# Backward attention loop: the dQ products of two neighbouring query chunks accumulate in one PSUM bank through zero-padded keys

## The chip, the cores and the metric

The kernel runs on one core of one Trainium2 chip. A core has TensorE (PE, with its weight loads listed apart as PEld), VectorE (DVE), ScalarE (ACT), GpSimd (POOL) and SyncE (SP), which run side by side and wait for each other through semaphores; DMA queues are fed from SP, ACT and POOL. The metric is device time in microseconds. The kernel before took 2488.68 us (median of three runs, 2481.41 to 2490.61).

## The reference, cut to what matters

The reference computes one transformer block with adaptive layer norm and all its gradients by `jax.vjp`. The sequence has 2048 tokens, the width is 512, and attention has 32 heads of 16 numbers each. The part that the change touches is the gradient through

```
scores = jnp.einsum('bhqd,bhkd->bhqk', q, k) * Dh ** (-0.5)
p = _softmax(scores, axis=-1)
o = jnp.einsum('bhqk,bhkd->bhqd', p, v)
```

With dS the gradient of the scores, this needs dQ = scale * dS K, dK = scale * dS^T Q and dV = P^T dO for each head, where P and dS are matrices of 2048 x 2048 that are never stored whole.

## The kernel before, in words

A forward part computes the output and the gradients of the dense layers. Then one backward loop goes over the attention matrices. Heads are taken in 8 groups of four (`hg`). For each group the loop goes over 4 chunks of 512 keys (`kc`), inside these over 4 chunks of 512 queries (`qc`), and inside these over 4 tiles of 128 queries (`qi`). One (hg, kc, qc) is called a block here: 128 blocks `b`, of four units each.

A block contains this work:

- `score` (L1594): 16 matmuls, one for each tile of queries and each head. Four heads lie in four groups of 32 rows. Each writes 128 x 512 scores to one PSUM bank: `psS_A`, `psS_B` or `psS_C`, on the tags `ps0`, `ps1` and `px`, one bank each.
- `expo` (L1600): 16 exponentials on ACT, each reading one such bank.
- `dp_pair` (L1614, L1616): 8 pairs of matmuls of dO with V into two banks (two such pairs of banks take turns), and on DVE one product of 128 x 1024 with the exponentials, which gives dS. The pair takes two of the four row groups: the even pairs of heads 0 and 1, the odd ones of heads 2 and 3.
- `k_quad` (L1654) and `v_quad` (L1663): four matmuls each, one for a head, in four groups of 32 columns, summing dK and dV of a key chunk in one bank, `accVK`. ACT copies it out once every four blocks (L1666).
- The transposes of dS: in even blocks DMA transposes, issued by SP (L1629, L1631), in odd blocks the last unit on PE (`pe_turn`, L1644, into bank C, copied out by ACT at L1760 in the block behind). A block's transposed dS is a tile `dsT`, of which there are three.
- `dq_quad` (L1681): four times four matmuls of a slice of K (32 columns, of which 16 are the head's own) with transposed dS, into one bank `dqacc` on the tag `px`, the same bank as `psS_C` and `ptT`.
- `dq_out` (L1691, L1694, L1699): ACT copies `dqacc` out once a block, to `dQacc` for the first key chunk and otherwise to `dqtmp`, which POOL adds to `dQacc`. `dQacc` has a column for each of the 2048 queries.

The engines' order is written out by hand. Two strings give it: `order_t` for even blocks b (whose predecessor used PE for its last transposes) and `order_n` for odd ones. Every engine takes its own instructions out of the string in that order, and waits in it. `s5` is the score 5 of the block, `e5` its exponential, `D` the next pair of dP matmuls with its DVE product (and with the DMA transposes that it makes possible), `q` the next K or V quad in turn, `t1` and `T1` the PE transposes and their copy, `f` a matmul that only keeps the array busy, `d1` and `d2` two dQ quads each, for the block two before, and `Q` its copy. The string of letters behind the order says which bank each score uses. Loads for the next head group are issued on ACT's queue at fixed counts of `D` (`at`, `plan_head`).

All of K lies in one tile `KS_tok` (16 tiles of 128 keys, 512 columns and 16 columns of zeros), loaded once before the loop from `k_st`.

Of the kernel before, what the change touches and what calls it, by code (L numbers as in the profile page):

```python
# [17 lines left out]
BF = dt.bfloat16  # L18
F32 = dt.float32

P = 128
# [9 lines left out]
QPAD = 528  # L31
# [3 lines left out]
def kernel(  # L35
# [54 lines left out]
    k_st = dram.tile([P, TT, D], BF, name="k_st")  # L90
# [56 lines left out]
    with ExitStack() as ph:  # L147
# [836 lines left out]
        def plan_tasks():  # L984
# [72 lines left out]
            def token_tile(which, g, ti):  # L1057
                key = (which, g)
                if ti == 0:
                    T[key] = cb.tile([P, 4, D], BF, name="tokP", tag=htags[(g if which == 0 else g + 1) % 3])  # L1060
                t = 4 * g + ti
                pt = pools["mm"].tile([P, 4, P], BF, name="ptk", tag="pm")
                for b in range(4):
                    src = sP[:, 4 + 4 * (g % 2) + b, ti * P:(ti + 1) * P] if which == 0 else KTs[b][:, t * P:(t + 1) * P]
                    PE.transpose(pt[:, b, :], src, identb[:])
                gs = slice(4 * g, 4 * g + 4)
                if which == 1:
                    DVE.tensor_copy(T[key][:, ti, :], pt.rearrange("p b q -> p (b q)"))
                    if ti == 3:
                        later(1, sp, k_st[:, gs, :], T[key][:])  # L1070
                else:
                    tok = T[key].rearrange("p t d -> p (t d)").rearrange("p (g t e) -> p g t e", g=HG, t=4)
                    DVE.tensor_copy(tok[:, :, ti, :], pt.rearrange("p b q -> p (b q)").rearrange("p (g e) -> p g e", g=HG))
                    if ti == 3:
                        later(1, sp, q_st.rearrange("g p t e -> p g t e")[:, :, gs, :], tok)
# [142 lines left out]

        def tick():
            unit[0] += 1  # L1220
            run_due()
            flush_sums()
            if dwq and unit[0] >= dwq[0][0]:
                next_chain()
# [8 lines left out]
        def last_chunk(O_c, L, w1T, w2T):  # L1233
# [127 lines left out]
            keep["KS"] = kpool.tile([P, TT, QPAD], BF, name="KS_tok", tag="ks")  # L1361
            POOL.memset(keep["KS"][:, :, D:QPAD], 0.0)
            for i in range(4):
                later(4 + 3 * i, sp, keep["KS"][:, 4 * i:4 * i + 4, 0:D], k_st[:, 4 * i:4 * i + 4, :])
# [171 lines left out]
    KS_tok, dOs_tok = keep["KS"], keep["dOs"]  # L1536
# [11 lines left out]
    with ExitStack() as ph:  # L1548
# [9 lines left out]
        def load_head(hg):  # L1558
            st = dict(hsets[hg % 2])
            st["qz"] = qz[hg % 2]  # L1560
            st["acc"] = stg.tile([P, n], F32, name="dQacc", tag="dQacc", bufs=1)
            st["dq"] = stg.tile([P, n], BF, name="dQst", tag="dQst", bufs=1)
            st["vk"] = stg.tile([P, n], BF, name="vkb", tag="vkb")
            hst[hg] = st
# [13 lines left out]
        def plan_head(hg):  # L1578
            j0 = (hg - 1) * 128 + 14
            loads = list(kvq_loads(hg)) + list(row_loads(hsets[hg % 2]["do"], dOT_st, hg, slice(0, n), d_st))  # L1580
            for i, (to, fro) in enumerate(loads):
                at(j0 + 4 * i, load, to, fro)
            at(j0 + 40, spread_qz, hg)

# [51 lines left out]
        def keep_warm():  # L1636
            PE.matmul(cur["vk"][0:DH, :], KS_tok[:, 0, D:QPAD], dOs_tok[:, 0, :], start=False, stop=False,
                      tile_position=(0, 0), skip_group_check=True)
# [34 lines left out]
        def dq_quad(b, kt):  # L1673
            hg, kc, qc, _ = units[4 * b]
            if kt == 0:
# [3 lines left out]
            for hq in range(4):  # L1679
                h = hg * 4 + hq  # L1680
                PE.matmul(acc[32 * hq:32 * hq + 32, :], KS_tok[:, kc * 4 + kt, h * DH:h * DH + 32], tT[:, :, hq * 4 + kt, :],  # L1681
                          start=(kt == 0), stop=(kt == 3), tile_position=(0, 32 * hq), skip_group_check=True)

        def dq_out(b):
            hg, kc, qc, _ = units[4 * b]
            acc = cur["dq"]
            del dqt[b]
            st = hst[hg]
            dst = st["acc"][:, qc * 512:(qc + 1) * 512]
            if kc == 0:  # L1690
                ACT.activation(dst, acc[:], AF.Identity, scale=SCALE)  # L1691
            else:
                tmp = wk.tile([P, 512], F32, name="dqtmp", tag="dqtmp")
                ACT.activation(tmp[:], acc[:], AF.Identity, scale=SCALE)  # L1694
                if kc == QC - 1:
                    dst2 = st["dq"][:, qc * 512:(qc + 1) * 512]
                else:
                    dst2 = dst
                POOL.tensor_tensor(dst2, dst, tmp[:], ALU.add)  # L1699
            if kc == QC - 1 and qc == QC - 1 and hg < HG - 1:  # L1700
                for hq in range(4):
                    r = hg % 2 * 64 + hq * DH
                    at(cur["j"] + 6 + hq, load, dQc[hg // 2, r:r + DH, :], st["dq"][32 * hq:32 * hq + DH, :])
# [4 lines left out]
            "s11 e10 D d1 d2 e11 Q q s12 D e12 s13 e13 q s14 D e14 "  # L1708
            "s15 q q e15 ").split(), "ABCABBABACABABCA"
        order_n = (  # L1710
            "s0 D s1 q e0 q s2 e1 e2 D s3 s4 q s5 e3 D e4 "
            "e5 s6 q s7 D s8 e6 e7 d1 e8 s9 D d2 e9 q Q s10 "
            "s11 e10 D q s12 e11 e12 s13 e13 D q s14 s15 e14 e15 D q ").split(), "CBACBACBABABCABC"
# [6 lines left out]
        with tc.manual_schedule(engines={PE.engine, ACT.engine, DVE.engine, SP.engine, POOL.engine}):  # L1720
# [4 lines left out]
            for b in range(NU // 4 + 3):  # L1725
                toks, bank = order_t if on_pe(b - 1) else order_n
                for tok in toks:
# [33 lines left out]
                    elif c == "d" and 0 <= b - 2 < NU // 4:  # L1761
                        for kt in (2 * i - 2, 2 * i - 1):
                            dq_quad(b - 2, kt)
                    elif c == "Q" and 0 <= b - 2 < NU // 4:
# [4 lines left out]
    with ExitStack() as ph:  # L1769
# [12 lines left out]
        for h in range(4):  # L1782
            SP.dma_start(out=xs["dq", 3][64 + DH * h:64 + DH * h + DH, :], in_=dq_last[32 * h:32 * h + DH, :])
# [238 lines left out]
```

## Time and profile before

| | |
|---|---|
| times of three runs | 2481.41, 2490.61, 2488.68 us; median 2488.68 |
| profiled execution, first to last instruction | 2501.3 us |
| mean granted TensorE clock | 0.980 of full speed |
| first and last exponential of the backward loop start at | 1115.7 and 2375.6 us |
| exponentials in the loop | 2048, medians 632 to 646 ns by bank |
| copies of `dqacc` | 128 (32 into `dQacc`, 96 into `dqtmp`), medians 597 ns |
| sums of dQ on POOL | 64 and 32, means 1268 and 1270 ns |

The profiled execution was 12.6 us longer than the median of the runs. Durations on ACT overlap: the next activation starts before the last one's recorded end, so the distance of two starts says what one costs, and the durations do not. The same holds for matmuls on PE.

### The profile page before, as it was taken

The page shows a single profiled execution, that of the slowest core. Times are in us where ns is not written, and L with a number is a line of the kernel's source. Part 1 is how long each engine was busy: PE and PEld are TensorE (multiplying, and loading weights), DVE is VectorE, ACT ScalarE, POOL GpSimd, SP SyncE. Part 2 cuts the span into 40 slices and gives each one's busy share as a digit, 9 for nine tenths or more (in the row PEclk, how much of TensorE's full clock was granted, in tenths as well). Part 3 has the DMA queues.
Part 4 walks back from the last instruction along what each step waited for, and adds up shares of the span by engine and source line. Part 5 has one row for each costly group of instructions (what it writes and reads, how often), then busy time and mean ns, then how long its engine had stood idle before and what let it go on. Part 6 is the DMA issues. An engine that isn't in the chain of part 4 may idle for free.

```text
span 2501.3 us, 49888 instructions
## 1 busy us (share of the span) xinstructions
PE 2324.0 (93%) x18948; PEld 783.4 (31%) x19036; DVE 1837.7 (73%) x2377; ACT 2303.7 (92%) x3560; POOL 488.0 (20%) x661
## 2 busy tenths in 40 slices
PE   8899899989998998999999999999999999999989
PEld 3232233223332333443223323233232323332344
DVE  6555354455435444579989999999999999999965
ACT  7999999999998999539999999999999999999944
POOL 2111223323533453110111101111011110110100
PEclk9999999999998999999999999999999999999999
DMA  4468463258546865979999999999999999999984
GB/s 146 130 167 176 144 150 97 88 166 142 98 95 142 151 131 110 256 200 196 201 192 206 199 198 202 196 204 203 205 205 198 205 202 199 200 198 214 201 253 133
DMA packets 1189503, 437.70 MB, mean 175 GB/s; under 512 B 1065867, under 2 KB 1160521, under 8 KB 1188878
## 3 DMA queue, kind: packets, MB, share of 16 engines
q1 hardware_dynamic: 1152414, 389.35, 79.0%
q0 software_dynamic: 19872, 27.09, 6.5%
q10 hardware_dynamic: 16976, 18.07, 2.9%
q8 instruction: 149, 2.44, 0.4%
q14 instruction: 92, 0.75, 0.1%
HBM read 98.30 MB, written 70.80 MB: 68 GB/s over the span
## 4 chain that ended last, share of the span: by engine, by line
ACT 40%; PE 38%; issue 8%; DVE 7%; DMA 3%; SPq 1%; ACTq 1%; POOL 0%; DVEq 0%; another core or an unknown queue 0%; POOLq 0%
ACT E_u L1600 24%; ACT ET L578 12%; PE dqacc L1681 4%; PE psST L576 3%; PE psS_A L1594 3%; PE accVK L1654 2%; PE pm L233 2%; ACT dsT L1760 2%; PE psS_B L1594 2%; PE pdh L1858 2%; PE oacc L592 2%; PE psS_C L1594 2%; PE pwq L1892 2%; PE pm L500 2%; PE pm L410 2%
## 5 line engine op out<-in xcount | busy, mean ns | idle before, releaser
L1616 DVE TENSOR_TENSOR dS_u<-psD_u,E_u 128x1024 bf16<-128x1024 f32 x1024 | 1185.9, 1218 | 77.1 <-PE psD_u L1614 30.2
L578 ACT ACTIVATE ET<-psST 128x1024 bf16<-128x1024 f32 x1024 | 941.9, 1242 | 16.6 <-PE psST L576 16.3
L1600 ACT ACTIVATE E_u<-psS_A 128x512 bf16<-128x512 f32 x768 | 509.9, 664 | 10.8 <-PE psS_C L1594 8.5
L1600 ACT ACTIVATE E_u<-psS_B 128x512 bf16<-128x512 f32 x768 | 503.2, 655 | 10.8 <-DMA dsT<-dS_u 2.7
L1614 PE MATMUL psD_u<-iv,ido 32*128 32x512 bf16 x2048 | 409.1, 388 | 1.5 <-DVE dS_u L1616 1.3
L576 PE MATMUL psST<-qt_sb,kt_sb 32*128 32x512 bf16 x2048 | 313.8, 386 | 48.0 <-ACT ET L578 41.0
L1600 ACT ACTIVATE E_u<-psS_C 128x512 bf16<-128x512 f32 x512 | 334.3, 653 | 3.1 <-PE psS_B L1594 1.1
L1594 PE MATMUL psS_B<-ik,iq 32*128 32x512 bf16 x768 | 296.1, 386 | 11.7 <-ACT E_u L1600 4.4
L1594 PE MATMUL psS_A<-ik,iq 32*128 32x512 bf16 x768 | 294.5, 383 | 11.0 <-DVE dwlast L237 1.0
L1699 POOL TENSOR_TENSOR dQacc<-dQacc,dqtmp 128x512 f32<-128x512 f32 x64 | 81.2, 1268 | 858.8 <-ACT dqtmp L1694 797.4
L1594 PEld LDWEIGHTS <-iq 32*128 32x128 bf16 x2048 | 129.7, 91 | 313.9 <-issue 296.9
L1654 PE MATMUL accVK<-dS_u,qz 128*32 128x512 bf16 x2048 | 213.5, 388 | 0.5 <-PE psD_u L1614 0.2
L592 PE MATMUL oacc<-ET,vaug 128*32 128x512 bf16 x2048 | 207.0, 394 | 3.9 <-DVE ostage L596 3.9
L1663 PE MATMUL accVK<-E_u,dOs_tok 128*16 128x512 bf16 x2048 | 204.5, 388 | 0.0
L1594 PE MATMUL psS_C<-ik,iq 32*128 32x512 bf16 x512 | 194.2, 379 | 4.5
L576 PEld LDWEIGHTS <-kt_sb 32*128 32x128 bf16 x2048 | 84.3, 91 | 328.2 <-issue 306.5
L1681 PE MATMUL dqacc<-dsT,KS_tok 128*32 128x512 bf16 x2048 | 145.7, 382 | 18.8 <-DMA dsT<-dS_u 5.0
L1760 ACT ACTIVATE dsT<-ptT 128x1024 bf16<-128x1024 bf16 x128 | 144.1, 1126 | 13.1 <-PE ptT L1644 12.2
L251 DVE COPY part<-pm 128x512 f32<-128x512 f32 (+2 forms) x106 | 65.2, 615 | 121.9 <-PE pm L233 111.8
L1614 PEld LDWEIGHTS <-ido 32*128 32x128 bf16 x2048 | 105.2, 91 | 101.3 <-issue 94.9
L1654 PEld LDWEIGHTS <-qz 128*32 128x32 bf16 x2048 | 58.5, 94 | 178.0 <-issue 162.9
L1699 POOL TENSOR_TENSOR dQst<-dQacc,dqtmp 128x512 bf16<-128x512 f32 x32 | 40.6, 1270 | 266.1 <-ACT dqtmp L1694 266.1
(415 smaller groups left out, 2688.7 us busy)
## 6 DMA issues: line engine op xcount, KB each, us to landing
p_st<-part POOLq DMA_DIRECT2D x36, 256.0 KB, 4.6
kt_sb<-qkT_st POOLq DMA_DIRECT2D x124, 64.0 KB, 3.0
wA<-in_B_w_dram SPq DMA_DIRECT2D x28, 256.0 KB
wB<-w1T_st SPq DMA_DIRECT2D x21, 256.0 KB
wA<-w2T_st SPq DMA_DIRECT2D x21, 256.0 KB
wB<-in_B_w_dram SPq DMA_DIRECT2D x21, 256.0 KB
p_st<-part POOLq DMA_DIRECT2D x28, 192.0 KB, 4.6
p_st<-part SPq DMA_DIRECT2D x18, 256.0 KB
```

Source lines behind the costliest of these rows:

```text
L576: PE.matmul(ps[:, hi, :], kt_sb[r:r + 32, kt * P:(kt + 1) * P], qt_sb[r:r + 32, :], start=True, stop=True, tile_position=(r, 0))
L578: ACT.activation(ET[:, 2 * pair:2 * pair + 2, :], ps[:], AF.Exp, scale=SCALE)
L592: PE.matmul(oacc[32 * hq:32 * hq + 32, :], lhsT, ET[:, hq, :], start=(kt == 0), stop=(kt == TT - 1), tile_position=(0, 32 * hq), skip_grou ...
L1594: PE.matmul(psS[:], st["q"][r:r + 32, qt * P:(qt + 1) * P], st["k"][r:r + 32, kc * 512:kc * 512 + 512], start=True, stop=True, tile_positi ...
L1600: ACT.activation(bst[u][0][:, hq, :], sst.pop((u, hq))[:], AF.Exp, scale=SCALE)
L1614: PE.matmul(psD[:, hi, :], st["do"][r:r + 32, qt * P:(qt + 1) * P], st["v"][r:r + 32, kc * 512:kc * 512 + 512], start=True, stop=True, til ...
L1616: DVE.tensor_tensor(dS_u[:, 2 * pair:2 * pair + 2, :], psD[:], E_u[:, 2 * pair:2 * pair + 2, :], ALU.mult)
L1654: PE.matmul(cur["vk"][32 * hq:32 * hq + 32, :], hst[hg]["qz"][:, qt, hq, :], bst[u][1][:, hq, :], start=(qt == 0), stop=False, tile_positi ...
L1663: PE.matmul(acc[32 * hq:32 * hq + DH, :], dOs_tok[:, qt, (hg * 4 + hq) * DH:(hg * 4 + hq + 1) * DH], E_u[:, hq, :], start=False, stop=(qt ...
L1681: PE.matmul(acc[32 * hq:32 * hq + 32, :], KS_tok[:, kc * 4 + kt, h * DH:h * DH + 32], tT[:, :, hq * 4 + kt, :], start=(kt == 0), stop=(kt ...
L1699: POOL.tensor_tensor(dst2, dst, tmp[:], ALU.add)
L1760: ACT.activation(dst, pt[:], AF.Identity)
```

## The change

One `dQacc` column now holds two queries. The 32 rows that a head has in `dqacc` are split: 16 rows for the even query chunk, 16 for the odd one. To this end each head's keys are laid out as 16 columns of zeros, 16 columns of keys, 16 of zeros (`KPAD` = 144 for four heads, `kpads`). A dQ quad of an even chunk takes 32 columns that begin with the keys, one of an odd chunk 32 columns that end with them. So the 8 quads of two neighbouring blocks sum into one bank, each adding zeros to the other's rows. One copy on ACT and, where there was one, one sum on POOL follow for both blocks.

- `dq_quad` is called once for each of `d1` to `d8`. All eight stand in `order_n`, that is in odd blocks: `d1` to `d4` for the block three before, `d5` to `d8` for the one two before. `Q` stands once, in `order_n` too. `order_t` has no `d` and no `Q` any more.
- The bank letters change: 4 instead of 3 scores of an even block, and 2 instead of 5 scores of an odd one use bank C.
- `dQacc` and `dQst` are half as wide. A head group's stores of dQ are 8 instead of 4 (`dq_stores`).
- K is stored by head group, and loaded for one group at a time (`ktok`), for the next one while one is worked on. POOL spreads it into the padded layout once for each group (`spread_keys`), into one of two buffers.

The number of matmuls does not change.

```diff
-                if which == 1:
-                    DVE.tensor_copy(T[key][:, ti, :], pt.rearrange("p b q -> p (b q)"))
-                    if ti == 3:
-                        later(1, sp, k_st[:, gs, :], T[key][:])
...
+                tok = T[key].rearrange("p t d -> p (t d)").rearrange("p (g t e) -> p g t e", g=HG, t=4)
+                DVE.tensor_copy(tok[:, :, ti, :], pt.rearrange("p b q -> p (b q)").rearrange("p (g e) -> p g e", g=HG))
+                if ti == 3:
+                    later(1, sp, (k_st if which else q_st).rearrange("g p t e -> p g t e")[:, :, gs, :], tok)
...
+        def split_keys():
+            flat_k = keep["KS"]
+            for i in range(2):
+                ktok.append(flat_k[:, i * TT * 64:(i + 1) * TT * 64].rearrange("p (t e) -> p t e", t=TT))
+                lo = 2 * TT * 64 + i * TT * KPAD
+                kpads.append(flat_k[:, lo:lo + TT * KPAD].rearrange("p (t c) -> p t c", t=TT))
+
+        def spread_keys(hg):
+            to = kpads[hg % 2][:, :, DH:].rearrange("p t (h c) -> p t h c", h=4)[:, :, :, 0:DH]
+            POOL.tensor_copy(to, ktok[hg % 2].rearrange("p t (h d) -> p t h d", h=4))
...
-            keep["KS"] = kpool.tile([P, TT, QPAD], BF, name="KS_tok", tag="ks")
-            POOL.memset(keep["KS"][:, :, D:QPAD], 0.0)
-            for i in range(4):
-                later(4 + 3 * i, sp, keep["KS"][:, 4 * i:4 * i + 4, 0:D], k_st[:, 4 * i:4 * i + 4, :])
+            keep["KS"] = kpool.tile([P, 2 * TT * (64 + KPAD)], BF, name="K_tok", tag="ks")
+            split_keys()
+            POOL.memset(keep["KS"][:, 2 * TT * 64:], 0.0)
+            later(4, sp, ktok[0], k_st[0])
+            later(9, spread_keys, 0)
...
+            at(j0 + 22, load, ktok[hg % 2], k_st[hg])
+            at(j0 + 50, spread_keys, hg)
...
-            if kt == 0:
+            odd = qc % 2
+            if kt == 0 and not odd:
                 cur["dq"] = psx.tile([P, 512], F32, name="dqacc", tag="px")
...
-                h = hg * 4 + hq
-                PE.matmul(acc[32 * hq:32 * hq + 32, :], KS_tok[:, kc * 4 + kt, h * DH:h * DH + 32], tT[:, :, hq * 4 + kt, :],
-                          start=(kt == 0), stop=(kt == 3), tile_position=(0, 32 * hq), skip_group_check=True)
+                lo = 32 * hq + (0 if odd else DH)
+                PE.matmul(acc[32 * hq:32 * hq + 32, :], hst[hg]["kpad"][:, kc * 4 + kt, lo:lo + 32], tT[:, :, hq * 4 + kt, :],
+                          start=(kt == 0 and not odd), stop=(kt == 3 and odd == 1), tile_position=(0, 32 * hq), skip_group_check=True)
...
-            dst = st["acc"][:, qc * 512:(qc + 1) * 512]
+            cols = slice(qc // 2 * 512, qc // 2 * 512 + 512)
+            dst = st["acc"][:, cols]
...
+        def dq_stores(to, fro):
+            for hq in range(4):
+                for half in range(2):
+                    yield (to[hq * DH:hq * DH + DH, :].rearrange("c (a e q) -> c a e q", e=2, q=512)[:, :, half, :],
+                           fro[32 * hq + DH * half:32 * hq + DH * half + DH, :].rearrange("c (a q) -> c a q", q=512))
...
             "s5 s6 e5 f f t2 e6 s7 T2 e7 D s8 e8 D f f s9 e9 q q s10 "
-            "s11 e10 D d1 d2 e11 Q q s12 D e12 s13 e13 q s14 D e14 "
-            "s15 q q e15 ").split(), "ABCABBABACABABCA"
+            "s11 e10 D e11 q s12 D e12 s13 e13 q s14 D e14 "
+            "s15 q q e15 ").split(), "ACBABBABACABCABC"
         order_n = (
             "s0 D s1 q e0 q s2 e1 e2 D s3 s4 q s5 e3 D e4 "
-            "e5 s6 q s7 D s8 e6 e7 d1 e8 s9 D d2 e9 q Q s10 "
-            "s11 e10 D q s12 e11 e12 s13 e13 D q s14 s15 e14 e15 D q ").split(), "CBACBACBABABCABC"
+            "e5 s6 q s7 D e6 s8 d1 e7 s9 d2 e8 s10 D d3 e9 s11 d4 q e10 "
+            "D s12 d5 e11 s13 d6 e12 s14 D d7 q e13 s15 d8 e14 Q e15 D q q ").split(), "ABCABCABABABABAB"
...
-                    elif c == "d" and 0 <= b - 2 < NU // 4:
-                        for kt in (2 * i - 2, 2 * i - 1):
-                            dq_quad(b - 2, kt)
-                    elif c == "Q" and 0 <= b - 2 < NU // 4:
+                    elif c == "d" and 0 <= b - 3 < NU // 4:
+                        dq_quad(b - 3 + (i > 4), (i - 1) % 4)
+                    elif c == "Q" and 0 <= b - 3 < NU // 4:
                         dq_out(b - 2)
```

## The prediction

> **What bounds the kernel now.** I read the engine table of the page first, then busy time by stage over the backward loop, then the timeline of 22 us in the middle of that loop. The first exponential of the loop starts at 1115.7 us and the last at 2375.6 us (the answer on the tile `E_u`): 1260 us for 128 blocks, 19.7 us for a pair. The change touches little outside this stretch.
>
> The page, and one stage of the loop (columns: window, length, then busy us of PE, weight loads, DVE, ACT, POOL, the granted clock, the DMA share, GB/s):
>
> ```profile
> span 2501.3 us, 49888 instructions
> ...
> PE 2324.0 (93%) x18948; PEld 783.4 (31%) x19036; DVE 1837.7 (73%) x2377; ACT 2303.7 (92%) x3560; POOL 488.0 (20%) x661
> ```
>
> ```profile
> 1600.00:1700.00 100.00, 96.04 (x938) 30.03 (x929) 95.35 (x83) 98.67 (x190) 11.62 (x8) 1.00 1.21 201
> ```
>
> Three engines look full here, so busy shares don't say which sets the pace. The timeline does (columns: start, duration, engine, line, operation):
>
> ```profile
> 1700.50 0.60 ACT L1600 ACTIVATE E_u<-psS_C 128x512 bf16<-128x512 f32 x1
> ...
> 1703.60 0.37 PE L1594 MATMUL psS_A<-ik,iq 32*128 32x512 bf16 x1
> ...
> 1704.09 0.61 PE L1681 MATMUL dqacc<-dsT,KS_tok 128*32 128x512 bf16 x8
> 1704.33 0.69 ACT L1600 ACTIVATE E_u<-psS_A 128x512 bf16<-128x512 f32 x1
> ...
> 1704.64 0.38 PE L1594 MATMUL psS_B<-ik,iq 32*128 32x512 bf16 x1
> 1704.64 0.39 PE L1614 MATMUL psD_u<-iv,ido 32*128 32x512 bf16 x2
> ...
> 1704.96 0.61 PE L1681 MATMUL dqacc<-dsT,KS_tok 128*32 128x512 bf16 x8
> 1705.06 0.60 ACT L1600 ACTIVATE E_u<-psS_B 128x512 bf16<-128x512 f32 x1
> ...
> 1705.40 0.39 PE L1654 MATMUL accVK<-dS_u,qz 128*32 128x512 bf16 x4
> 1705.68 0.60 ACT L1694 ACTIVATE dqtmp<-dqacc 128x512 f32<-128x512 f32 x1
> ...
> 1705.72 0.39 PE L1594 MATMUL psS_A<-ik,iq 32*128 32x512 bf16 x1
> ...
> 1706.18 0.59 ACT L1600 ACTIVATE E_u<-psS_A 128x512 bf16<-128x512 f32 x1
> ...
> 1706.65 0.61 ACT L1600 ACTIVATE E_u<-psS_B 128x512 bf16<-128x512 f32 x1
> ...
> 1709.04 0.67 ACT L1600 ACTIVATE E_u<-psS_A 128x512 bf16<-128x512 f32 x1
> ...
> 1709.42 0.59 PE L1614 MATMUL psD_u<-iv,ido 32*128 32x512 bf16 x2
> ...
> 1711.42 1.17 ACT L1760 ACTIVATE dsT<-ptT 128x1024 bf16<-128x1024 bf16 x1
> ...
> 1712.33 0.75 ACT L1600 ACTIVATE E_u<-psS_B 128x512 bf16<-128x512 f32 x1
> ...
> 1716.01 1.05 PE L1681 MATMUL dqacc<-dsT,KS_tok 128*32 128x512 bf16 x16
> ...
> 1716.62 0.80 ACT L1600 ACTIVATE E_u<-psS_B 128x512 bf16<-128x512 f32 x1
> ...
> 1717.16 0.76 ACT L1694 ACTIVATE dqtmp<-dqacc 128x512 f32<-128x512 f32 x1
> ...
> 1717.65 0.75 ACT L1600 ACTIVATE E_u<-psS_A 128x512 bf16<-128x512 f32 x1
> ...
> 1719.84 0.60 ACT L1600 ACTIVATE E_u<-psS_C 128x512 bf16<-128x512 f32 x1
> ```
>
> Read starts against starts. Number the exponentials of a block e0 to e15 and their scores s0 to s15. An odd block (written by `order_n`) runs from 1700.50 to 1709.04, 8.54 us; the even block behind it (`order_t`) to 1719.84, 10.80 us: 19.34 us a pair. From the lines come these prices:
>
> - ACT starts an undisturbed exponential every 0.48 us (1706.18, 1706.65). The copy of `dqacc` holds it 0.50 us (1705.68 to 1706.18), a copy of `ptT` 0.91 us (1711.42 to 1712.33).
> - PE starts a further quad of the same kind 0.22 us after the one before: four quads take 1.05 us, of which the last is a matmul's 0.39, and (1.05 - 0.39)/3 = 0.22. From a score to a quad it takes 0.32 us (1704.64 to 1704.96), from a quad to a score 0.32 us too (1705.40 to 1705.72). Elsewhere in the same timeline both are 0.31 (1700.11 to 1700.42, 1700.65 to 1700.97), which I use.
> - Scores and dP matmuls start together when they read different 32-row groups (s9 and a dP pair, both 1704.64, the pair over in 0.39). When they share a group, the pair takes 0.59 (1709.42): 0.20 more.
> - A score starts 0.05 us after the exponential that empties its bank, and an exponential 0.04 after its score (1704.64 + 0.38, then 1705.06).
>
> ACT is nearly gapless (16 x 0.48 = 7.63 of an odd block's 8.54), PE waits for banks and so has some spare time, DVE needs 16 x 1.14 = 18.2 of a pair's 19.34. The loop is bound by ACT, with PE just able to feed it. Where it is not, the cost shows: s8, d1 (two quads), s9 takes 1.04 us, and e9 starts 0.73 after e8, not 0.48 (s8 to d1 is 0.49 there, 0.18 over the plain change, as d1 waits for bank C).
>
> **What the change takes away.** Of each pair, one `dqacc` copy on ACT. In the even block e11 to e12 is 1.03 us (1716.62 to 1717.65); without the copy 0.48, so -0.55. The four quads go from there too (1.05 us of PE); they stand beside the copy, and if they also caused the 0.28 us that the next block's e0 is late (1719.08 to 1719.84 is 0.76), up to -0.83. I take -0.55, since s15 and two quads behind it stay as they are. One of two POOL sums (1.27 us) goes: nothing, POOL is 12% busy in this stage.
>
> **What it moves.** All eight quads of a pair of blocks now stand in the odd block, one at a time, between s8 and the block's end; and their accumulator keeps bank C, so that s6 to s15 have A and B alone. Two banks by themselves: 0.38 + 0.04 + 0.60 + 0.05 = 1.07 us for two exponentials, 0.53 for one, 0.05 above ACT's own pace. But PE cannot keep even that: score, quad, score is 0.31 + 0.31 = 0.62. The string runs one D behind the blocks, so a block's first D is an odd pair (rows 64 and 96), its fifth and seventh too. Step by step, on PE, start to start:
>
> - s8 to s9, s9 to s10: 0.62 each.
> - s10 to s11: 0.62, and a dP pair in rows 64 and 96 beside s10, which is in row 64: +0.20, 0.82.
> - s11 to s12: d4, a K quad, a dP pair (rows 0, 32), s12 (row 0): 0.31 + 0.22 + 0.31 + 0.20 = 1.04.
> - s12 to s13, s13 to s14: 0.62 each.
> - s14 to s15: dP pair (row 64 again), d7, a V quad: 0.20 + 0.31 + 0.22 + 0.31 = 1.04.
> - s15 to the next s0: d8, dP pair, K quad, V quad, s0: 0.31 + 0.31 + 0.31 + 0.22 + 0.31 = 1.46.
>
> Together 6.84 us from s8 to the next s0, and so from e8 to the next e0. Before it, e0 to e8 as now (1700.50 to 1704.33 is 3.83) plus 0.11 as s8 waits for the end of e6 instead of e5: 3.94. The odd block takes 10.78 us where it took 8.54: +2.24. The copy in it stands behind d8: e15 starts 0.31 + 0.39 + 0.05 + 0.50 = 1.25 us after s15, and the next e0 could follow at 1.73; s0 allows it at 1.46 + 0.42 = 1.88. So the copy's wait lies beside PE's work and is next in line should PE be quicker.
>
> A pair: +2.24 - 0.55 = +1.69 us, 21.0 in all, above the 18.2 that DVE needs, so DVE does not set it. 63 pairs have quads beside exponentials (the 64th drains behind the last exponential, as now): 63 x 1.69 = +106.
>
> **A rule of the skill.** The rows price a change between scores and quads at 0.31 where two quads are 0.22 apart. The Trainium skill, TensorEngine Tiling (Array Packing), section Tiling Modes, Key Properties, says that a change of tiling mode drains the engine; it gives no figure. Taken as a wait for the whole matmul it would speak against this change more than the rows do (last rival below); the trace agrees that a change costs, and only with the smaller price.
>
> **Smaller parts.** The transposes for an odd block reuse the buffer that d1 to d4 of that block read, so SP's queue waits for d4, some 2 us; behind it are the other transposes, which d5 wants two blocks later. Bounds 0 and 63 x 0.3 us (a slip of one switch); I take 0. Eight stores a head for four, and one key load: 35 more issues on ACT's queue. One at 1701.56 took 0.31 and the exponentials around it (1701.47, 1701.95) kept 0.48; bounds 0 to 35 x 0.31 = 11, I take 0. POOL spreads the keys once a head, like the `qz` spread of 2.77 us, with most of a head's time to do it; its first memset grows from 0.31 us to about 4 (a 2048-column one takes 1.80), some 40 us before the loop, hidden. The stores of K in smaller pieces lie in the forward half, four of them, where the page's slices show DMA 40 to 80% busy: between 0 and 2 us, taken as 0. None of these gains anything, as none shortens a queue that ACT or PE waits for.
>
> **Sum.** The profiled execution has a span of 2501.3 us, 12.6 above the median of 2488.7; 2501 + 107 = 2608 in its terms (106, and 1 for the drain), 2488.7 + 107 = 2596 as a median.
>
> **Rivals.**
>
> - *Faster: ACT keeps the pace.* ACT is 98.7% busy, and 64 copies of 0.50 us go: -32, 2457 us. It holds if a score comes back within 0.48 us with a quad between. For it: scores wait for banks today, so PE has slack on the average. Against: s8 to s9 takes 1.04 us with two quads between; 0.18 of it is d1's wait for bank C and 0.22 the second quad, so 0.62 to 0.64 is left for one. The Trainium skill, same page, Performance Considerations, PSUM Bottleneck, says that under tiling the copies out of PSUM may become the limit, which would favour this rival; ACT's share agrees, the late e9 does not. 0.07.
> - *No change: banks alone.* The quads vanish in the waits for banks and ten exponentials pay 0.05: +0.55 a pair against -0.55. 2489 us. 0.05.
> - *A smaller loss.* Single quads switch for 0.25, halfway to 0.22, so that plain scores come at the banks' 0.53: s8 to s0 is 4 x 0.53 + 0.73 + 2 x 0.92 + 1.22 = 5.91, the pair +1.31 - 0.55 to -0.83, +30 to +48: about 2528. No row shows 0.25. 0.13.
> - *A full drain.* Each of 18 changes from s8 to s0 waits for the matmul's end, 0.39 for 0.31: +1.4 a pair more, 2687 us. Today's rows speak against it. 0.05.
> - *The sum above:* 2596, with its own range 2550 to 2620 (two of three row clashes that cost nothing, -25; the extra -0.28, -18; switches 0.02 dearer, +23). 0.70.
>
> The range 2520 to 2630 leaves out the first two rivals and the full drain. 12 us, 0.5%, is about what can be told from no change here: faster 0.07, same 0.05, slower 0.88.
>
> **What the changed profile would show.** 64 copies of `dqacc` for 128, at unchanged 0.6 us; odd blocks near 10.8 us and even ones near 10.2; in odd blocks exponentials 0.62 apart from e8 and over 1 us apart at e11 to e12, in the timeline; ACT's share in the loop down to about 90%, DVE's to 88%; loads and POOL unnoticed. Wrong if e8 to e14 keep 0.48: then PE had time that I have booked twice, or a quad between scores costs less than today's rows say.

## The result, and the profile after

The changed kernel takes 2706.28 us (median of 6 runs, 2701.68 to 2713.48). The kernel before took 2489.64 us (6 runs, 2481.41 to 2492.01). The ratio is 1.087, with a 95% interval of 1.085 to 1.089: slower, by 217 us. The forecast was 2596 us, at most 2630. The direction was right. The loss is twice as large as forecast.

The page of the changed kernel, its first lines and the row of the granted TensorE clock (40 slices of 67.7 us, in tenths of full speed):

```profile
span 2706.9 us, 49707 instructions
...
PE 2467.9 (91%) x18948; PEld 774.7 (29%) x19036; DVE 1858.3 (69%) x2377; ACT 2328.5 (86%) x3496; POOL 439.6 (16%) x621
...
PEclk9999999999989999999899899798898997998999
```

ACT has 64 instructions fewer (3560 to 3496), the 64 copies. The profile has 18948 matmuls as before, and yet PE is busy for 144 us more. The last row gives a reason: from the middle of the span on, one slice in two or three shows 8 or 7. The loop (first to last exponential) now takes 1468.4 us, from 1117.0 to 2585.4. Before it took 1259.9. That is 208.5 us more, and the two profiled spans differ by 205.6, so the loss is all in the loop.

Busy time by stage in the changed kernel (window, length, busy us of PE, weight loads, DVE, ACT, POOL, then the granted clock, the DMA share, GB/s):

```profile
1300.00:1400.00 100.00, 90.36 (x709) 23.06 (x705) 74.61 (x63) 77.91 (x141) 6.29 (x4) 0.83 0.97 163
1400.00:1500.00 100.00, 93.63 (x845) 26.16 (x845) 87.46 (x76) 90.45 (x167) 6.34 (x5) 1.00 1.04 183
1500.00:1600.00 100.00, 90.65 (x737) 24.10 (x736) 77.40 (x66) 80.75 (x146) 6.29 (x4) 0.88 0.94 170
```

There are two kinds of stage. The middle one runs at full clock, with ACT at 90.45% and DVE at 87.46%: the forecast said "about 90%" and 88%. In the stages on either side PE does 709 and 737 matmuls for 845, at a clock of 0.83 and 0.88.

**The undisturbed stage.** The timeline of one odd block there (start, duration, engine, line, operation; in brackets the idle time before and what ended it):

```profile
1444.71 0.64 ACT L1612 ACTIVATE E_u<-psS_A 128x512 bf16<-128x512 f32 x1
...
1448.35 0.37 PE L1606 MATMUL psS_A<-ik,iq 32*128 32x512 bf16 x1 [0.31 <-ACT E_u L1612]
...
1448.65 0.40 PE L1694 MATMUL dqacc<-dsT,K_tok 128*32 128x512 bf16 x4
1448.76 0.60 ACT L1612 ACTIVATE E_u<-psS_A 128x512 bf16<-128x512 f32 x1
...
1448.98 0.38 PE L1606 MATMUL psS_B<-ik,iq 32*128 32x512 bf16 x1
...
1449.63 0.38 PE L1606 MATMUL psS_A<-ik,iq 32*128 32x512 bf16 x1
...
1450.49 0.39 PE L1606 MATMUL psS_B<-ik,iq 32*128 32x512 bf16 x1
...
1451.58 0.37 PE L1606 MATMUL psS_A<-ik,iq 32*128 32x512 bf16 x1
...
1453.94 0.39 PE L1606 MATMUL psS_B<-ik,iq 32*128 32x512 bf16 x1
...
1455.46 0.38 PE L1606 MATMUL psS_A<-ik,iq 32*128 32x512 bf16 x1
...
1455.88 0.60 ACT L1612 ACTIVATE E_u<-psS_A 128x512 bf16<-128x512 f32 x1
```

The scores shown are s8, s9, s10, s11, s12, s15 and the next s0. Score to quad is 0.30 us (1448.35 to 1448.65), quad to score 0.33 (1448.65 to 1448.98): the forecast's 0.31 each. s8 to s9 takes 0.63, s9 to s10 0.65, s10 to s11 0.86, s11 to s12 1.09, and s15 to the next s0 1.52. The forecast had 0.62, 0.62, 0.82, 1.04, 1.46. From s8 to s0 it is 7.11 us against 6.84, and the block takes 11.17 (1444.71 to 1455.88) against 10.78.

**The other stages.** At each of the seven changes of head group lies a stretch like the one that follows. First the chain of work of the changed kernel around the first of them (start, us, what the time went to; ACTq and SPq are the queues on which ACT and SP issue transfers, L1586 is where `load` issues):

```profile
1318.99 8.68 DMA dsT<-dS_u
1327.69 0.33 ACTq L1586
1328.06 1.22 ACTq L1586
1329.38 0.60 ACT E_u L1612
...
1332.67 0.55 PE dqacc L1694 x4
1333.22 0.53 PE psS_A L1606
1333.75 0.43 PE psD_u L1626 x2
1334.18 0.55 PE dqacc L1694 x4
```

Then the timeline of the same place:

```profile
1318.99 11.03 SPq L1643 DMA_TRANSPOSE dsT<-dS_u  x2
...
1320.66 1.17 ACTq L1586 DMA_DIRECT2D dQc<-dQst  x1
...
1321.92 1.28 ACTq L1586 DMA_DIRECT2D dQc<-dQst  x1
...
1323.80 1.05 ACTq L1586 DMA_DIRECT2D dQc<-dQst  x1
...
1325.54 0.37 PE L1606 MATMUL psS_A<-ik,iq 32*128 32x512 bf16 x1
...
1327.69 0.33 ACTq L1586 DMA_DIRECT2D iqs<-q_st  x1
1328.06 1.22 ACTq L1586 DMA_DIRECT2D dQc<-dQst  x1
1329.38 0.60 ACT L1612 ACTIVATE E_u<-psS_B 128x512 bf16<-128x512 f32 x1 [3.90 <-issue]
...
1330.03 0.58 PE L1606 MATMUL psS_B<-ik,iq 32*128 32x512 bf16 x1 [3.80 <-ACT E_u L1612]
```

The eight stores of dQ stand between the exponentials in ACT's instruction stream, one after every D. The four shown take 1.05 to 1.28 us each to issue. A load of `iqs` between them comes only when a transpose on SP's queue has landed: the trace has semaphore 110 on both, so the issue waits for an earlier transfer whose semaphore it uses again. No exponential starts until 1329.38, 3.90 us later than ACT could, and PE stands still for 3.80 us (1326.23 to 1330.03), waiting for the bank. Its clock falls to half at 1326.8, 0.6 us into that, and stays there for 34.1 us: a score takes 0.53 to 0.58 us, not 0.37, and a quad 0.55, not 0.40. An odd block, which PE paces now, takes 20.6 us there instead of 11.4. The four blocks from the change of head group take 11.7, 20.6, 14.8 and 11.7, together 58.7; four undisturbed ones take 42.8. That is +15.9; the other six changes cost 12.8, 15.8, 14.3, 12.8, 13.5 and 13.3. Sum: 98 us.

In all, the loop spent 198.0 us at half clock after its first 12 us. Before, it was 47.8 us, in 13 short stretches.

### The profile page after: what moved, and what is told of

Its sections match the earlier page's. It is cut to its first block, busy times and chain, and to the rows that moved or that the text cites. A ratio compares the mean times of both kernels' runs of the same rounds, so it can differ in the third digit from the quotient of the medians.

```text
span 2706.9 us, 49707 instructions
## 1 busy us (share of the span) xinstructions
PE 2467.9 (91%) x18948; PEld 774.7 (29%) x19036; DVE 1858.3 (69%) x2377; ACT 2328.5 (86%) x3496; POOL 439.6 (16%) x621
## 4 chain that ended last, share of the span: by engine, by line
PE 51%; ACT 29%; issue 7%; DVE 7%; DMA 3%; ACTq 1%; POOL 1%; another core or an unknown queue 0%; SPq 0%; DVEq 0%; POOLq 0%
ACT E_u L1612 14%; ACT ET L578 12%; PE dqacc L1694 7%; PE psS_A L1606 6%; PE psS_B L1606 5%; PE psD_u L1626 4%; PE accVK L1666 4%; PE psST L576 3%; PE accVK L1675 3%; PE psS_C L1606 2%; DMA dsT<-dS_u 2%; ACT dsT L1776 2%; PE ptT L1656 2%; PE pm L233 2%; PE pdh L1873 2%
## 5 line engine op out<-in xcount | busy, mean ns | idle before, releaser
L1628 DVE TENSOR_TENSOR dS_u<-psD_u,E_u 128x1024 bf16<-128x1024 f32 x1024 | 1206.7, 1219 | 264.4 <-PE psD_u L1626 221.0
L1626 PE MATMUL psD_u<-iv,ido 32*128 32x512 bf16 x2048 | 436.5, 402 | 0.0
L1606 PE MATMUL psS_B<-ik,iq 32*128 32x512 bf16 x832 | 334.9, 402 | 60.2 <-ACT E_u L1612 56.1
L1606 PE MATMUL psS_A<-ik,iq 32*128 32x512 bf16 x832 | 330.5, 397 | 27.9 <-ACT E_u L1612 22.9
L1612 ACT ACTIVATE E_u<-psS_C 128x512 bf16<-128x512 f32 x384 | 236.6, 616 | 14.5 <-PE psD_u L1626 3.9
L1666 PE MATMUL accVK<-dS_u,qz 128*32 128x512 bf16 x2048 | 230.8, 404 | 19.7 <-ACT vkb L1678 16.2
L1694 PE MATMUL dqacc<-dsT,K_tok 128*32 128x512 bf16 x2048 | 215.7, 413 | 1.0 <-DMA dsT<-dS_u 1.0
L1710 POOL TENSOR_TENSOR dQacc<-dQacc,dqtmp 128x512 f32<-128x512 f32 x32 | 40.6, 1268 | 923.4 <-ACT dqtmp L1708 923.4
L1606 PE MATMUL psS_C<-ik,iq 32*128 32x512 bf16 x384 | 151.1, 393 | 8.9 <-ACT E_u L1612 6.6
L1776 ACT ACTIVATE dsT<-ptT 128x1024 bf16<-128x1024 bf16 x128 | 131.1, 1024 | 13.0 <-PE ptT L1656 12.6
L1694 PEld LDWEIGHTS <-K_tok 128*32 128x32 bf16 x2048 | 52.9, 93 | 215.0 <-issue 210.7
```

The lines of the kernel that those rows point to most:

```text
L1606: PE.matmul(psS[:], st["q"][r:r + 32, qt * P:(qt + 1) * P], st["k"][r:r + 32, kc * 512:kc * 512 + 512], start=True, stop=True, tile_positi ...
L1612: ACT.activation(bst[u][0][:, hq, :], sst.pop((u, hq))[:], AF.Exp, scale=SCALE)
L1626: PE.matmul(psD[:, hi, :], st["do"][r:r + 32, qt * P:(qt + 1) * P], st["v"][r:r + 32, kc * 512:kc * 512 + 512], start=True, stop=True, til ...
L1628: DVE.tensor_tensor(dS_u[:, 2 * pair:2 * pair + 2, :], psD[:], E_u[:, 2 * pair:2 * pair + 2, :], ALU.mult)
L1666: PE.matmul(cur["vk"][32 * hq:32 * hq + 32, :], hst[hg]["qz"][:, qt, hq, :], bst[u][1][:, hq, :], start=(qt == 0), stop=False, tile_positi ...
L1694: PE.matmul(acc[32 * hq:32 * hq + 32, :], hst[hg]["kpad"][:, kc * 4 + kt, lo:lo + 32], tT[:, :, hq * 4 + kt, :], start=(kt == 0 and not od ...
```

## The experiments

The two theories at the start. *Order*: all of the loss is PE's order in the odd block, and only its prices were set too low. *Boundaries*: the steady order costs about what was forecast, and the rest comes from the eight stores on ACT's queue. They differ in what spreading the stores does.

### Where the second half comes from: the stores

The stores at wider distances, one in eight D:

```diff
-                    at(cur["j"] + 6 + i, load, to, fro)
+                    at(cur["j"] + 6 + 8 * i, load, to, fro)
```

> The changed kernel, with its eight stores of dQ after each head group issued one every eight D instead of one every D; nothing else. In the trace of the changed kernel the blocks 2 to 4 of each head group take 55 to 59 us with their neighbour where four blocks take 42.8 elsewhere, and the TensorE clock is at half for 24 to 34 us there. Theory A: the stores stand close together on ACT's queue and each waits for the landing of an earlier transfer, a transpose of dS among them; ACT and then PE stand still, the clock halves, and seven groups lose about 14 us each. Then this kernel takes 2706 - 80 to 98 = 2608 to 2626 us, and the long half-clock stretches go. Theory B: it is other work at the start of a group (the key load, POOL's spreading) or the thin PE work of the odd blocks that halves the clock. Then it stays within 2690 to 2710.

Measured 2613.93 us, ratio to before 1.050 (1.045 to 1.055). The same eight stores at their old places, issued by POOL instead of ACT:

```diff
-                    at(cur["j"] + 6 + i, load, to, fro)
+                    at(cur["j"] + 6 + i, POOL.dma_start, to, fro)
```

> The changed kernel, with the same eight stores at the same places but on POOL's queue instead of ACT's. Theory A (ACT's queue is held by them): 2605 to 2626 us, as with the stores spaced out, since POOL is 16% busy and nobody waits for it soon. Theory A' (the transfers themselves crowd the DMA engines or SP's transposes): the boundary still costs over 8 us for each group, 2665 or more. Theory B: 2690 to 2710.

Measured 2611.42 us, 1.049 (1.043 to 1.055). Both take 92 to 95 us away. The clock row of the page with the stores apart, and the busy times of the stage that had 0.83:

```profile
PEclk9999999999999999979999999999999999999999
```

```profile
1300.00:1400.00 100.00, 93.26 (x844) 26.16 (x843) 88.27 (x76) 91.00 (x168) 6.29 (x4) 1.00 1.09 190
```

844 matmuls at a clock of 1.00 instead of 709 at 0.83, and every block regular: even ones 9.9 or 10.3 us, odd ones 11.2 or 11.4, across the changes of head group too. One stretch of 17.1 us at half clock is left, at the loop's start. An issue of such a store takes 0.567 us in the median, at most 0.68; in the changed kernel 0.710, at most 1.30. So the second half of the loss lies in eight close issues on ACT's queue. The transfers themselves are not to blame, since on POOL's queue they follow as closely and cost nothing. How much of it is the issue time and how much the wait for an earlier transfer no run separates: both edits take away both. The trace of the changed kernel says only how the stand-stills of ACT are made up. The longest at each of the seven changes take 2.7 to 4.8 us, together 24.4; issues fill 11.3 of these, and in the other 13.1 ACT waits ahead of an issue.

Do eight stores cost that much without the new order? The kernel before, each of its four stores cut in two column halves, one after every D:

```diff
-                    at(cur["j"] + 6 + hq, load, dQc[hg // 2, r:r + DH, :], st["dq"][32 * hq:32 * hq + DH, :])
+                    for half in range(2):
+                        part = slice(n // 2 * half, n // 2 * half + n // 2)
+                        at(cur["j"] + 6 + 2 * hq + half, load, dQc[hg // 2, r:r + DH, part], st["dq"][32 * hq:32 * hq + DH, part])
```

> The kernel before, with each of its four stores of dQ per head group split into two halves of the columns, so eight stores, one every D. Theory A with ACT alone: ACT is held as in the changed kernel, about 14 us a group, +60 to +100 us (2550 to 2590). Theory A with PE's slack: the kernel before catches up, as PE is not the limit of its odd blocks and the clock comes back at once: less than +25 us. Theory B: no difference.

Measured 2517.91 us, 1.011 (1.002 to 1.021): a loss between 5 and 51 us, less than the 92 whichever end holds. Its loop spends 37.5 us at half clock, no more than before. These issues, each of one run of columns, take 0.508 us in the median. Pieces and order both differ from the changed kernel, so this run doesn't say which of them makes the stores dearer there.

The kernel before has such a stand-still once, with its own four stores. An issue of one waits for a transpose, and ACT and PE stop for 2.72 and 2.29 us:

```profile
1774.28 0.60 ACT L1600 ACTIVATE E_u<-psS_A 128x512 bf16<-128x512 f32 x1
...
1777.22 0.32 ACTq L1576 DMA_DIRECT2D dQc<-dQst  x1
1777.59 0.60 ACT L1600 ACTIVATE E_u<-psS_B 128x512 bf16<-128x512 f32 x1 [2.72 <-DMA dsT<-dS_u]
...
1778.24 0.37 PE L1594 MATMUL psS_B<-ik,iq 32*128 32x512 bf16 x1 [2.29 <-ACT E_u L1600]
```

That block takes 13.99 us where its like take 10.6. Half clock follows at 1779.8, for 3.4 us. In the run with eight stores the longest stand-still of PE takes 3.08 us (from 1942.2) and comes with 3.4 us at half clock too; no stretch at half clock there is longer than 10.2. In the changed kernel the stand-stills of PE are 2.6 to 4.7 us long, and the half clock lasts 24 to 34. So in the old order the clock came back sooner than in the new one.

The next run asks what the clock costs in the changed kernel: twelve matmuls that add zero, ahead of s7 in the odd block after the change of head group, where PE would stand still.

```diff
+                    if tok == "s7" and b % 16 == 3 and 16 < b < NU // 4:
+                        for _ in range(12):
+                            keep_warm()
```

> The changed kernel, its stores untouched, with twelve matmuls that add zeros (2.6 us of PE) ahead of s7 in block 3 of each head group but the first, where PE stands still for 3.9 us in the trace because ACT is held. If the fall of the clock to half is what the stand-still of PE brings, and not something the stores do, the clock stays up in most groups and a boundary costs 5 instead of 14 us: about 2706 - 45 to 65 = 2641 to 2661. If the clock falls anyway, or ACT's own wait is most of the 14 us: 2700 to 2725.

Measured 2668.05 us, 1.071 (1.068 to 1.074): 38 us less than the changed kernel, with work added. The time at half clock falls from 198.0 to 85.3 us. It lies between the two forecasts, as the matmuls came at the right moment in some head groups and not in others. In a group where the clock stayed up, the four blocks take 11.6 + 15.1 + 10.3 + 11.2 = 48.2 us, +5.4 over the undisturbed 42.8. So of some 14 us that a change of head group costs, about 5 are the stand-still and 9 the half clock behind it: 7 x 14 = 98.

### What the steady part is made of

With the stores apart the changed kernel is still 124 us slower than before (2613.93 - 2489.85, the time before measured beside it), where the forecast had 107. Three terms of it can be undone alone. The row clashes: the last four D moved by a score or two, so that no dP pair stands beside a score of its own 32 rows.

```diff
-            "e5 s6 q s7 D e6 s8 d1 e7 s9 d2 e8 s10 D d3 e9 s11 d4 q e10 "
-            "D s12 d5 e11 s13 d6 e12 s14 D d7 q e13 s15 d8 e14 Q e15 D q q ").split(), "ABCABCABABABABAB"
+            "e5 s6 q s7 D e6 s8 d1 e7 s9 D d2 e8 s10 d3 e9 s11 D d4 q e10 "
+            "s12 d5 e11 s13 D d6 e12 s14 d7 q e13 s15 D d8 e14 Q e15 q q ").split(), "ABCABCABABABABAB"
```

> The changed kernel, with the last four D of the odd block moved so that no dP pair starts beside a score of its own row groups (D with s9, s11, s13 and s15 instead of s10, s12, s14 and the end); nothing else. If PE's order sets the odd block, as the prediction's sum has it: s8 to the next s0 goes from 6.84 to 5.84 us (0.62 x 5 + 0.84 x 2 + 1.06), 1.0 us a pair, 63 us in all: about 2643. If the waits between ACT and PE over two banks set it instead, less than 15 us: over 2690.

> The changed kernel with both edits: D moved off the scores of its own row groups, and the stores of dQ one every eight D. If the steady pair (21.4 us, the PE order) and the group boundaries (the stores on ACT's queue) are two separate costs, they go separately: the pair is that of the run with D moved, 9.9 + 10.65 and 10.3 + 10.4, 20.6 for 21.4, and no long half-clock stretch: 2614 - 64 x 0.75 = 2566 us. If the stores' cost had hung on PE being the limit, it would be lower still.

The second run is this edit with the stores apart. Measured 2630.92 us (1.057, 1.051 to 1.063) and 2569.82 us (1.034, 1.028 to 1.039). The cleaner comparison is the latter with the stores apart alone: 44 us less by the medians, 40 by the ratios. The odd block falls from 11.29 to 10.51 us in the mean, the even one rises from 10.09 to 10.21; 0.66 x 64 = 42. The three clashes were forecast at 0.60.

The bank alone, in the kernel before: s12 and s15 of the odd block taken off bank C, so that the scores from s7 on have A and B (from s6 on in the changed kernel). The quads stay where they are.

```diff
-            "s11 e10 D q s12 e11 e12 s13 e13 D q s14 s15 e14 e15 D q ").split(), "CBACBACBABABCABC"
+            "s11 e10 D q s12 e11 e12 s13 e13 D q s14 s15 e14 e15 D q ").split(), "CBACBACBABABABAB"
```

> The kernel before with one edit: s12 and s15 of the odd block use banks A and B instead of C, so that from s8 on two banks alternate. Copies, quads and their places are as before. If two banks cost only the longer cycle (1.07 us for two exponentials, 0.05 each) it is 6 x 0.05 = 0.3 us a pair, +20 us, 2510. If the third bank is what lets PE do quads and dP pairs while ACT works, each of these runs shows as a late exponential: +0.7 us a pair or more, +45, 2535 or more.

Measured 2591.6 us, 1.042 (1.037 to 1.048): +105 (the kernel before, measured beside it: 2486.23), for an edit that moves no instruction and adds none. Its timeline where the clock is full, in an odd block:

```profile
1854.32 0.60 ACT L1600 ACTIVATE E_u<-psS_A 128x512 bf16<-128x512 f32 x1
...
1854.81 0.59 ACT L1600 ACTIVATE E_u<-psS_B 128x512 bf16<-128x512 f32 x1
...
1855.37 0.60 ACT L1600 ACTIVATE E_u<-psS_A 128x512 bf16<-128x512 f32 x1
...
1855.87 0.59 ACT L1600 ACTIVATE E_u<-psS_B 128x512 bf16<-128x512 f32 x1
```

Two exponentials in 1.05 us; the forecast worked out 1.07. So the cycle of two banks is as worked out. At full clock it costs more than the 0.3 us a pair expected for this run: odd and even block together +0.49 us in the median, 0.49 x 64 = 31 us. The other 74 us are in the clock row of its page and in a stage of its loop:

```profile
PEclk9999999999999999999888989988889979878999
```

```profile
1800.00:1900.00 100.00, 94.27 (x826) 27.22 (x822) 85.65 (x74) 91.17 (x169) 10.17 (x7) 0.86 1.03 181
```

273.1 us at half clock, in 27 stretches, and even blocks of 12.29 us in the mean where their median is 10.88. The Trainium skill, TensorE: Matmul & The Clock Gate, section "A second HAM failure mode: psum-queue depth-cycling", describes a kernel whose TensorE idles briefly while it cycles through PSUM banks, and whose clock goes up and down for it; this run agrees, with 0.939 as the execution's mean clock against 0.980 before. It too has the median matmul at its full-clock length and the loss in stretches: here the scores into bank C take 0.384 us in the median and up to 0.629. In the windows of 3.4 us ahead of most falls PE is busy for 0.81 to 0.83 of the time, with no gap over 0.39 us, against 0.95 to 0.97 in the windows before them.

What the copies are worth, in the kernel before: 48 of the 128 copies and their sums skipped.

```diff
+            if qc % 2 == 0 and kc > 0:
+                if kc == QC - 1:
+                    POOL.tensor_copy(st["dq"][:, qc * 512:(qc + 1) * 512], dst)
+                return
```

> The kernel before without the copy of dqacc (and without its sum on POOL) for the even query chunks of the last three key chunks: 48 of 128 copies are left out, so dQ lacks these parts; matmuls, banks and order are unchanged. It shows what the copies are worth by themselves. By the prediction's price (0.55 us each in the even block) -26 us: about 2463. If the copies stand beside something else, no difference: 2485 to 2495.

Measured 2489.83 us, 1.002 (0.999 to 1.005): no difference. The timeline of this run, at e11 and e12 of an even block without a copy:

```profile
1530.33 1.05 PE L1681 MATMUL dqacc<-dsT,KS_tok 128*32 128x512 bf16 x16
...
1530.74 0.59 ACT L1600 ACTIVATE E_u<-psS_B 128x512 bf16<-128x512 f32 x1
...
1531.19 0.40 PE L1654 MATMUL accVK<-dS_u,qz 128*32 128x512 bf16 x4
...
1531.53 0.38 PE L1594 MATMUL psS_A<-ik,iq 32*128 32x512 bf16 x1
...
1531.95 0.60 ACT L1600 ACTIVATE E_u<-psS_A 128x512 bf16<-128x512 f32 x1 [0.61 <-PE psS_B L1594]
```

The four quads and a K quad now end the wait: s12 cannot start before 1531.53, and e12 comes 1.21 us after e11. The median over the even blocks is 0.99, and with the copy it was 1.04. The reverse, three of the four quads of each even block skipped and the copy kept:

```diff
-                          start=(kt == 0), stop=(kt == 3), tile_position=(0, 32 * hq), skip_group_check=True)
+                          start=(kt == 0), stop=(kt == (3 if b % 2 else 0)), tile_position=(0, 32 * hq), skip_group_check=True)
...
-                            dq_quad(b - 2, kt)
+                            if b % 2 or kt == 0:
+                                dq_quad(b - 2, kt)
```

> The kernel before with three of the four dQ quads of every even chunk left out (48 matmuls of 64 in four blocks, so dQ lacks these parts); the copy of dqacc stays. Without the copies the kernel before took the same time (2489.8 against 2486.2). Theory: copy and quads of the even block lie side by side between e11 and e12, each hiding the other, so this alone is worth little too: e11 to e12 keeps 0.48 + 0.50 = 0.98, 0 to 0.1 us a pair, 2480 to 2490 us. If PE's quads were the whole cost there, and the copy only beside them, e11 to e12 falls to 0.6 or less: -0.4 us a pair, 2460.

Measured 2476.15 us, 0.995 (0.991 to 0.999): 13 us less, a little more than expected. e11 to e12 is 0.95, twice 0.48: now the copy alone holds it. Every second even block is 0.26 us shorter (10.38 for 10.64 in the median), some 8 us in all, and the profiled loop has 17.1 us at half clock for 47.8. In the changed kernel, where copy and quads are both gone from the even block, e11 to e12 is 0.48. So they lay beside each other there: each is worth little while the other is there, and only both together are worth the 0.55 us.

### Can the new layout be ordered well?

Both order strings of the changed kernel rewritten, with the stores apart: the quads in runs (d1 to d4 as two pairs, d5 to d7, d8), three banks for the scores between the runs.

```diff
         order_n = (
...
-            "e5 s6 q s7 D e6 s8 d1 e7 s9 d2 e8 s10 D d3 e9 s11 d4 q e10 "
-            "D s12 d5 e11 s13 d6 e12 s14 D d7 q e13 s15 d8 e14 Q e15 D q q ").split(), "ABCABCABABABABAB"
+            "D s0 e0 s1 e1 q s2 e2 s3 D q s4 q e3 D e4 s5 s6 e5 s7 D d1 d2 e6 d3 d4 e7 s8 s9 D d5 d6 e8 e9 d7 D s10 s11 d8 e10 q q e11 D s12 s13 q Q e12 e13 s14 e14 q s15 e15 D q ").split(), "BACBACABBABAABCA"
```

> The changed kernel, spaced stores, with both order strings written anew: the eight dQ quads stand in runs (d1 to d4, d5 to d7, d8 with a K and a V quad) between pairs of scores that start together, no dP pair beside a score of its own rows, the copy three exponentials before the block's end. Nine runs of quads in the odd block instead of twelve: 3 x (0.31 + 0.31 - 0.22) = 1.2 us less, no clashes 0.75 less, the late copy hidden: 21.4 - 1.95 = 19.45 us a pair or a little less, 2614 - 125 = 2489, with 2465 to 2515 about it. If holding bank C for the quads costs the same wherever they stand, it stays over 2560.

Measured 2578.69 us, 1.038 (1.034 to 1.041): 90 us above what was expected. One pair of blocks in two takes 10.0 + 9.4 = 19.4 us, as little as planned. The other, in which `accVK` is copied out, takes 11.2 + 9.3 even at full clock, as PE waits for that copy behind two exponentials:

```profile
1376.38 0.62 ACT L1678 ACTIVATE vkb<-accVK 128x512 bf16<-128x512 f32 x1
...
1377.04 0.38 PE L1649 MATMUL accVK<-dOs_tok,K_tok 128*16 128x512 bf16 x1 [1.41 <-ACT vkb L1678]
```

Four blocks at full clock take 39.9 us for 38.5 in the kernel before (medians by their place among the four), 1.4 x 32 = 44 us in all. The clock row of its page shows the rest:

```profile
PEclk9999999999999999998989898998999899999899
```

191.1 us at half clock in 26 stretches. They touch 26 of 31 even blocks with that wait (the loop's first left out) and none of the even blocks without it. So this order loses at full clock and through the clock, about half each. The time is over the 2560 of the other theory, but the blocks without the wait are as short as planned, and the wait is for the copy of `accVK`, not for bank C.

Last, the kernel before with its own clock kept up, by two more zero-adding matmuls (`f`) in each even block:

```diff
-            "s0 s1 q s2 e0 e1 D s3 D e2 s4 e3 t1 e4 q T1 D "
+            "s0 s1 q f s2 e0 e1 D s3 D f e2 s4 e3 t1 e4 q T1 D "
```

> The kernel before with two more of its matmuls that only keep the array busy in each even block, behind the first quad and behind the second dP pair. Its clock falls to half for 3.4 us some fourteen times in the loop, always in the window that ends 2 us into an even block, and such a block takes 12.0 us for 10.7. If the two matmuls prevent that, -14 x 1.3 = -18 us; each of them costs PE 0.2 us where it is late already, up to 64 x 0.2 = +13. So 2468 to 2500.

Measured 2484.8 us over 10 runs, 0.998 (0.997 to 1.000). Behind the loop's first 12 us no time at half clock is left (47.8 us before); an even block at full clock is 0.1 to 0.2 us longer for the added matmuls. With 6 to 13 us paid, and a loop 15 us shorter, the half clock had cost the kernel before about 21 to 28 us. That holds for the two profiled executions, and the one of the kernel before was 12.6 us above its median; by the medians the gain is 4 us. It is the fastest full version that ran, by 0.2%.

## Why the prediction was off, point by point

- *The step that failed* is in "Smaller parts": "35 more issues on ACT's queue ... bounds 0 to 35 x 0.31 = 11, I take 0". Measured: 92 us (2706.28 against 2613.93 with the stores apart), 98 us by the blocks. It failed twice. The price came from one lone load of 0.31 us, while eight two-piece stores, one per D, took 0.71 each in the median, issues in the same queue waited for earlier transfers, and ACT's next exponentials stood behind them. A row nearer to the case stood in the trace before: the store at 1777.22, with ACT held for 2.72 us. And no step had a term for the TensorE clock, which made about 9 of each 14 us. The row of the clock on the page before was all nines but one, and behind that store it showed only 3.4 us at half: a reason for such a term, but not for its size.
- *"What it moves"* was right in mechanism, by the timeline, and short in size. Odd block +2.24 forecast; +2.75 measured at full clock (11.29 against 8.54), 32 us over 63 pairs. A step from score to quad to score was 0.01 to 0.03 dearer, e0 to e8 took 4.05 for 3.94, and every second odd block is 0.24 us longer (11.41 for 11.17), for which there was no term. The row clashes (0.60 a pair) measured 0.66.
- *"What the change takes away"*: -0.55 forecast, -0.61 measured (10.09 against 10.70). The reason given was wrong in part. The copy by itself is worth nothing; the gain needed the quads to go as well, which the forecast mentioned only for a further 0.28.
- *The pair* is thus +2.14, for +1.69 forecast, or 63 x 2.14 = 135 us at full clock. The steady part came out at 116 in the loop, nearer to 106 than its terms, because the kernel with the stores apart has lost the stretches at half clock that cost the kernel before some 20 to 28 us in its profiled execution. The agreement of that sum owes something to two errors of opposite sign.
- *"The loop is bound by ACT, with PE just able to feed it"* overstated ACT. Skipping 48 copies of 0.48 us, 23 us of ACT's time, changed nothing. At 98.7% busy ACT would still have waited for PE at e11 to e12, where the copies stood.
- *The rivals.* "ACT keeps the pace" fell, with s8 to s9 at 0.63. "Banks alone" had its price nearly right at full clock (+0.49 a pair for +0.55) but not its claim that the quads vanish, with s8 to s9 at 0.63 and not 0.53. In the old order two banks cost 105 us, some 74 of them through the clock; the changed kernel with its stores apart has two banks there as well and a single stretch of 17.1 us at half clock, so those 74 are no part of its loss. "A smaller loss" needed switches of 0.25 and they are 0.30 to 0.33. "A full drain" at 2687 us has the number nearest to the result and is still refuted: a score or quad does not wait for the 0.39 to 0.40 of the one before, so the Trainium skill's rule (TensorEngine Tiling (Array Packing), Tiling Modes, Key Properties) that a change of mode drains the engine shows here as 0.08 to 0.11 us over the 0.22 of two quads, as the forecast had it.
- *The signs*: 64 copies of 0.60 us, even blocks near 10.2, exponentials 0.62 apart (0.63 to 0.65), over 1 us at e11 to e12 (1.08), ACT's and DVE's shares came as named; odd blocks "near 10.8" were 11.2 to 11.4. "Loads and POOL unnoticed" did not hold for what ACT issues.

What stays open: why the clock goes down where it does in the two-bank and in the rewritten orders, with gaps of some 0.4 us at most ahead of its falls in the one and a wait of 1.4 us in the other, and why it stays down for 24 to 34 us in the changed kernel. That two banks make PE and ACT wait for each other often enough to count as idle is argued from the two-bank run; no run changed the idle time alone in those blocks. Nor did a run take away the changes between scores and quads and leave the rest: that term of the steady loss is read from the timeline.

## What to carry to other kernels

Price an issue on a compute engine's queue by what stands behind it in that engine's stream, and look at the row of its nearest like (same pieces, same distance to the next issue), not at a lone transfer. Where two engines hand each other banks and TensorE sets the pace, a stand-still of a few microseconds can be paid again through the clock, as at the seven changes here, so put a line for the granted clock in the sum, and look at which block would be hit. Taking an operation off a busy engine gains only if nothing else fills the same gap: find what ends the wait next before booking it.

## What was not expected of the hardware

- A PE stand-still of 3.80 us came with 34.1 us at half clock, through blocks that PE paced. The Trainium skill, TensorE: Matmul & The Clock Gate, section "HAM oscillation — how this bites in real kernels", warns of gaps of over about 3.4 us, after which TensorE goes to half clock. The trace agrees in part: the clock fell 0.6 us into this stand-still, and two of the other six, of 2.6 and 2.7 us, brought a fall as well. The same page, section "What's actually happening", has the clock return after one busy window of that length; here the return took seven to ten times as long. With the stores apart the same blocks kept full clock.
- Two banks for three, without another instruction, cost 4.2% in the old order, of which about 1.2% shows at full clock (31 us).
- The issue of a store by ACT took 0.38 us in the median in the kernel before, 0.57 in two pieces far apart, 0.71 in two pieces close together. The longest took 2.08 us in the kernel before, and 0.68 and 1.30 in these two. Issued on POOL's queue, the stores left the blocks as short as with the stores apart.
